# Loads, conversions and sums of logarithms moved in a fused attention and feed-forward kernel

## The chip, the cores and the metric

The kernel runs on one core of a Trainium2 chip. The core has a matrix engine (TensorE, PE in the profile, with weight loads shown as PEld), a vector engine (VectorE, DVE), a scalar engine (ScalarE, ACT), a general engine (GpSimd, POOL) and a synchronisation engine (SyncE, SP) that here issues most of the transfers. Transfers are carried by 16 DMA engines. The metric is the device time of one execution in microseconds (us).

## The reference

Two blocks run one after the other. The first is a gated linear recurrence over 768 positions, for 4 batches and 8 heads of 48 values:

```python
for t in range(S):
    state = alpha[:, :, t, :, None] * state + np.einsum('bhd,bhe->bhde', k[:, :, t], v[:, :, t])
    y[:, :, t] = np.einsum('bhd,bhde->bhe', q[:, :, t], state)
```

Its output, seen as 3072 tokens of 384 values, goes through a multiplicative feed-forward block:

```python
a = x @ w1          # 384 x 1024
b = x @ w2          # 384 x 1024
h = a * b @ w3      # 1024 x 1024
return (h @ w_out)  # 1024 x 384
```

q, k, v and alpha are float32; the four weights arrive as float64 and are read as 64-bit words.

## The kernel before, in words

**Chunks.** The positions are cut into chunks of 128: six to a batch, 24 in all (N). Within a chunk the recurrence becomes matrix products. `logs(n)` takes the logarithm of alpha on ScalarE (L233); `decays(n)` sums the logarithms along the chunk with one matmul by a triangular matrix, `utri` for odd and `after` for even chunks (L241), and ScalarE takes two exponentials of the sums (L244, L245); `decayed(n)` multiplies k and q by them on VectorE (L253); `transposed(n)` transposes both on TensorE (L272) and copies them out of PSUM on ScalarE (L273); `scores(n)` multiplies them (L311) and VectorE masks the result (L314); `outer(n)` and `advance(n)` carry the state; `attend(n)` forms the output (L330, L333), which ScalarE copies (L337) and stores to a buffer `xd` in DRAM (L343). The loop runs these functions for different chunks at once: in iteration n, `logs` works on chunk n+4, `decays` on n+3, `decayed` on n+2, `transposed` on n+1.

**Gates.** Three chunks make a group of 384 tokens. `load_x(g)` loads a group's x from `xd` into the tile xT, of which there is one (L348). `split_x(g, i)` splits it into three float32r parts: one on ScalarE (L354), two on VectorE (L355, L356), which follow each other. A gate, `gate(g, f)`, computes 128 columns of a and b for a group: twice `exact`, with six matmuls (L365), an eviction by ScalarE (L367), three more matmuls (L369) and an addition on VectorE (L370); then the product of the two (L381), stored to DRAM later (L388). `run(1)` does half a gate, one of its two `exact`s. `begin` says in which iterations a group starts: 4, 8, 12, 16 and 20, each with four gates (the last with all eight). So between two starts there are eight halves, two to an iteration.

**Conversion.** The float64 weights are turned into float32 with integer and float instructions (`to_fp32`, L184 to L194). For w1 and w2 there are twelve units (`load_gates`): each loads 2 x 256 KB (L176) and then takes four steps, the last of which write the three float32r parts (L202 to L205). `convert(steps)` advances units by so many steps. It keeps up to three units begun, that is, loaded; after a step it puts the unit back in the second place, so that two units take turns. The iterations have 3 steps up to chunk 2 and 4 after that, until the 48 steps are done. There are three buffers for the raw words.

**Order.** Loads of q, k, v, alpha, of the raw weights and of x are all issued by SP, in one queue; stores of x and of a few rows for the state (`ends`) by ScalarE. Each engine executes its instructions in a fixed order, which a scheduler sets when the program is built. The order of the text gives precedence; work that is ready is taken ahead of work that isn't. The trace shows this: the loads of w_out, which the text has after the loop, are issued from 114.76 us on.

**After the loop** the remaining gates run, mixed with the conversion of w_out and w3 and with the product w3 @ w_out (`fold`, L408 to L419), and at last `project` multiplies the stored products of a and b by that (again L365 and L369, with w3o and ab).

## Time and profile before

| | |
|---|---|
| median of 6 runs | 510.61 us (507.64 to 511.32) |
| the profiled execution, its own time | 510.45 us |
| its span, first to last instruction | 508.7 us |
| TensorE busy, matmuls and weight loads | 479.6 us (94%) and 427.5 us (84%) |
| VectorE busy | 365.6 us (72%) |
| ScalarE busy | 245.7 us (48%) |
| GpSimd busy | 12.4 us (2%) |
| DMA | 79.07 MB, 155 GB/s over the span |

The span has three stages. The loop over chunks ends at about 217 us, the remaining gates and folds at about 404 us, the projection at the end. Busy shares are averages over these stages, which have different limits. A matmul's time in the groups is longer than its share of a full pipeline: in the chain of work, six gate matmuls follow each other in 1.04 us.

### The profile page before, as it was taken

What the parts mean: (1) busy time and instruction counts of PE and PEld (TensorE: products, weight loads), DVE (VectorE), ACT (ScalarE), POOL (GpSimd) and SP (SyncE); (2) the same over time, 40 slices, a digit from 0 to 9 for tenths busy, and PEclk for the clock granted to TensorE, in tenths of its full rate; (3) what the DMA queues carried; (4) which work ended last, traced back from release to release, by engine and by line L of the source; (5) the groups of instructions that cost most, each with busy time, mean ns of one, the idle gap of its engine ahead of it and who ended that gap; (6) DMA issues with size and microseconds to landing.
All of it is one profiled execution on the core that took longest, in us unless ns stands there. A gap on an engine that the chain in (4) does not pass through costs nothing.

```text
span 508.7 us, 9463 instructions
## 1 busy us (share of the span) xinstructions
PE 479.6 (94%) x3568; PEld 427.5 (84%) x3568; DVE 365.6 (72%) x606; ACT 245.7 (48%) x465; POOL 12.4 (2%) x41
## 2 busy tenths in 40 slices
PE   3877699999899999999999999999999999999996
PEld 2655588787788888899999988898889899999996
DVE  2778799997746556499999986967434597777661
ACT  3665667666445544355555545454223433333330
POOL 1001000000000000000000000000000000000000
PEclk9989599999899999999999999999999999999999
DMA  9989999999886733165665543322100786555511
GB/s 175 181 208 204 241 214 234 236 247 231 239 147 144 156 78 98 46 185 166 198 195 162 170 158 103 125 82 69 46 32 32 197 228 193 178 175 176 172 49 46
DMA packets 168733, 79.07 MB, mean 155 GB/s; under 512 B 112856, under 2 KB 162544, under 8 KB 168688
## 3 DMA queue, kind: packets, MB, share of 16 engines
q1 hardware_dynamic: 149184, 73.68, 57.0%
q10 hardware_dynamic: 19504, 4.80, 4.8%
q8 instruction: 28, 0.46, 0.4%
q14 instruction: 17, 0.14, 0.1%
HBM read 56.40 MB, written 22.06 MB: 154 GB/s over the span
## 4 chain that ended last, share of the span: by engine, by line
PE 74%; DVE 0%; issue 0%; DVEq 0%
PE bank L365 36%; PE bank L369 18%; PE bank L414 8%; PE bank L333 2%; PE bank L272 2%; PE bank L311 2%; PE bank L408 1%; PE bank L330 1%; PE bank L283 1%; PE bank L241 1%; DVE o L370 0%; DVEq L370 0%
## 5 line engine op out<-in xcount | busy, mean ns | idle before, releaser
L365 PE MATMUL bank<-x,w 128*128 128x384 f32 x768 | 164.1, 348 | 9.6 <-ACT x L354 8.2
L365 PEld LDWEIGHTS bank<-x,w 128*128 128x128 f32 x768 | 134.5, 190 | 15.4 <-ACT x L354 8.6
L367 ACT ACTIVATE t<-bank 128x384 f32<-128x384 f32 x152 | 74.2, 491 | 129.5 <-PE bank L365 98.7
L370 DVE SCALAR_TENSOR_TENSOR r<-bank,t 128x384 f32<-128x384 f32 x128 | 69.1, 553 | 49.6 <-ACT t L367 44.4
L369 PE MATMUL bank<-x,w 128*128 128x384 f32 x384 | 88.3, 337 | 1.0 <-DVE x L356 0.9
L369 PEld LDWEIGHTS bank<-x,w 128*128 128x128 f32 x384 | 68.6, 189 | 2.3 <-DVE x L356 1.6
L365 PE MATMUL bank<-w3o,ab 128*128 128x384 f32 x384 | 70.4, 334 | 0.0
L365 PEld LDWEIGHTS bank<-w3o,ab 128*128 128x128 f32 x384 | 66.9, 188 | 0.0
L414 PE MATMUL bank<-wo,w3T 128*128 128x384 f32 x128 | 42.6, 486 | 0.0
L184 ACT ACTIVATE rest<-raw 128x512 f32<-128x512 uint32 (+1 forms) x36 | 23.5, 653 | 33.8 <-DMA raw<-in_moe_w_dram 32.2
L369 PE MATMUL bank<-w3o,ab 128*128 128x384 f32 x192 | 37.1, 334 | 0.0
L414 PEld LDWEIGHTS bank<-wo,w3T 128*128 128x128 f32 x128 | 24.2, 189 | 14.9
L381 DVE TENSOR_TENSOR ab<-r 128x384 f32<-128x384 f32 x64 | 35.5, 555 | 1.0
L314 DVE TENSOR_TENSOR ms<-bank,keep 128x512 int32<-128x512 int32 x48 | 30.9, 682 | 7.4 <-PE bank L311 7.4
L433 DVE TENSOR_TENSOR ab<-abl,ab 128x1024 fp32r<-128x1024 f32 x24 | 29.4, 1224 | 9.2 <-ACT ab L432 9.2
L432 ACT ACTIVATE ab<-abl 128x1024 fp32r<-128x1024 f32 x24 | 25.5, 1063 | 18.8 <-PE bank L369 18.8
L273 ACT COPY qkT<-bank 128x512 f32<-128x512 f32 x48 | 26.1, 588 | 16.1 <-PE bank L272 13.7
L369 PEld LDWEIGHTS bank<-w3o,ab 128*128 128x128 f32 x192 | 33.6, 188 | 0.0
L311 PE MATMUL bank<-qkT 48*128 48x128 f32 x384 | 28.9, 292 | 4.9 <-ACT qkT L273 4.9
L272 PE MATMUL bank<-ident,qk 128*128 128x128 f32 x192 | 29.3, 302 | 3.9 <-DVE qk L253 3.9
L311 PEld LDWEIGHTS bank<-qkT 48*128 48x128 f32 x384 | 24.2, 193 | 10.2 <-ACT qkT L273 6.8
L253 DVE TENSOR_TENSOR qk<-kq,e 128x768 f32<-128x768 f32 x24 | 22.9, 952 | 12.3 <-ACT e L245 7.5
(59 smaller groups left out, 499.7 us busy)
## 6 DMA issues: line engine op xcount, KB each, us to landing
abd<-ab SPq DMA_DIRECT2D x64, 192.0 KB
abl<-abd SPq DMA_DIRECT2D x24, 512.0 KB
raw<-in_moe_w_dram SPq DMA_DIRECT2D x16, 512.0 KB
xT<-xd SPq DMA_DIRECT2D x12, 576.0 KB
raw<-in_moe_w_dram SPq DMA_DIRECT2D x24, 256.0 KB
ac<-in_alpha_dram SPq DMA_DIRECT2D x24, 192.0 KB
kq<-in_k_dram SPq DMA_DIRECT2D x24, 192.0 KB
kq<-in_q_dram SPq DMA_DIRECT2D x24, 192.0 KB
```

Source lines behind the costliest of these rows:

```text
L272: nc.tensor.transpose(tp[:, ds(j * C, C)], qk[:, i, 2 * j:2 * j + 2, :], ident)
L273: nc.scalar.copy(qkT[:, i], tp.rearrange("p (j c) -> p j c", j=NP))
L311: nc.tensor.matmul(sc[i][:, j, :], qkT[r, 0, j, :], qkT[r, 1, j, :], start=True, stop=True)
L314: nc.vector.tensor_tensor(ms[:, i].bitcast(I32), sc[i].bitcast(I32), keep_bc, op=ALU.bitwise_and)
L365: nc.tensor.matmul(p1, w[part][i], x[part][i], start=(part == i == 0), stop=(part == 1 and i == n - 1))
L367: nc.scalar.activation(t, p1, AF.Copy, scale=(1.0 + 1.0 / P) * scale)
L369: nc.tensor.matmul(p2, w[2][i], x[2][i], start=(i == 0), stop=(i == n - 1))
L370: nc.vector.scalar_tensor_tensor(to, p2, -scale, t, op0=ALU.mult, op1=ALU.add)
L381: nc.vector.tensor_mul(ab, *r)
L414: nc.tensor.matmul(po, w3T[:, j, :], wo[:, j, :], start=(j == 0), stop=(j == KF - 1))
L432: nc.scalar.activation(t[:, 0], ab, AF.Copy, scale=1.0 - 2.0 ** -13)
L433: nc.vector.tensor_sub(t[:, 1], ab, t[:, 0].bitcast(FP32))
```

## The change

The diff has four parts.

- `decays(n)` for chunks from `LATE` = 10 on uses float32r. `logs` splits the logarithms into a rounded part (a copy on ScalarE) and the rest (a subtraction on VectorE), both in one tile `la2` with one buffer; `decays` makes two float32r matmuls in place of one in float32. The triangular matrices are copied once into float32r on GpSimd.
- `convert` puts a unit back in the first place, so that one unit is finished before the next is started; up to three are still loaded ahead.
- The steps of an iteration change: 3 up to chunk 2 and 4 for chunks 3 to 6, at partly other places; from chunk 7 on one, and one more in every third chunk. With the first step before the loop this makes 1 + 9 + 16 + 22 = 48 in all, the last in chunk 23.
- In the loop `load_x` is issued by ScalarE, in the iteration in which the group starts instead of at the end of the one before. The split stands in the iteration after that, behind `scores`; the first half gate of that iteration moves to its end. After the loop x is loaded by SP, as before.

```diff
+    LATE = 10
...
+    sums = p1.tile([C, 2, C], FP32R, name="sums")
...
+    nc.gpsimd.tensor_copy(out=sums[:, 0], in_=after)
+    nc.gpsimd.tensor_copy(out=sums[:, 1], in_=utri)
...
                 next(x)
-                begun.insert(min(1, len(begun)), x)
+                begun.appendleft(x)
...
-        st["la", n] = work.tile([C, DM], FP32, tag="la", name="la")
-        nc.scalar.activation(st["la", n], a, AF.Ln)
+        la = st["la", n] = work.tile([C, DM], FP32, tag="la", name="la")
+        nc.scalar.activation(la, a, AF.Ln)
+        if n >= LATE:
+
+            t = st["la", n] = work.tile([C, 2, DM], FP32R, tag="la2", name="la2", bufs=1)
+            nc.scalar.copy(t[:, 0], la)
+            nc.vector.tensor_sub(t[:, 1], la, t[:, 0].bitcast(FP32))
...
-        nc.tensor.matmul(lc, utri if n % 2 else after, st.pop(("la", n)), start=True, stop=True)
+        la = st.pop(("la", n))
+        if n < LATE:
+            nc.tensor.matmul(lc, utri if n % 2 else after, la, start=True, stop=True)
+        else:
+            for i in range(2):
+                nc.tensor.matmul(lc, sums[:, n % 2], la[:, i], start=(i == 0), stop=(i == 1))
...
-    def load_x(g):
+    def load_x(g, queue=nc.sync):
         st["xT", g] = xp.tile([C, KM, TG], FP32, tag="xT", name="xT")
-        nc.sync.dma_start(out=st["xT", g], in_=xd[g].rearrange("(k p) t -> p k t", p=C))
+        queue.dma_start(out=st["xT", g], in_=xd[g].rearrange("(k p) t -> p k t", p=C))
...
         scores(n)
+        if n - 1 in begin:
+            g, tiles = begin[n - 1]
+            split_x(g, 0)
+            fill.extend(gate(g, f) for f in tiles)
         if n == 0:
             logs(2)
             decays(2)
             logs(3)
+        early = n < 7
         convert(1, 2 if n == 0 else 3)
-        run(1)
+        run(n - 1 not in begin)
         advance(n)
         outer(n)
+        if early:
+            convert(1)
         transposed(n + 1)
         decayed(n + 2)
         logs(n + 4)
-        convert(1 if n < 3 else 2)
+        if n in begin:
+            load_x(begin[n][0], nc.scalar)
+        convert(early and n > 2)
         run(1)
         decays(n + 3)
         load_ends(n + 2)
-        convert(1)
-        if n in begin:
-            g, tiles = begin[n]
-            split_x(g, 0)
-            fill.extend(gate(g, f) for f in tiles)
+        convert(early or n % 3 == 0)
         attend(n)
-        if n + 1 in begin:
-            load_x(begin[n + 1][0])
+        run(n - 1 in begin)
     part1.close()
```

## The prediction

> **What bounds the kernel now.** I read the page's forty slices first, then the windows by stage, the waits, and the order of time around the worst gaps. The slices (12.7 us each; tenths of busy time, tenths of granted clock, busy share of the DMA engines):
>
> ```profile
> PE   3877699999899999999999999999999999999996
> PEclk9989599999899999999999999999999999999999
> DMA  9989999999886733165665543322100786555511
> ```
>
> TensorE is full from the eleventh slice to the end. The idle time lies in the first ten, where the DMA engines are full too. The windows (each engine's busy us and count, then TensorE's clock, DMA share, GB/s) show it by stage:
>
> ```profile
> 24.00:36.00 12.00, 8.03 (x118) 6.40 (x114) 7.99 (x15) 7.83 (x16) 0.91 (x3) 0.94 0.93 211
> 48.00:60.00 12.00, 4.21 (x15) 3.00 (x12) 9.20 (x14) 5.34 (x11) 0.00 (x0) 0.66 0.99 215
> 84.00:96.00 12.00, 11.42 (x123) 9.16 (x122) 11.30 (x19) 6.70 (x13) 0.77 (x2) 1.00 1.09 227
> 120.00:132.00 12.00, 9.53 (x78) 7.08 (x77) 11.41 (x22) 7.61 (x17) 0.69 (x2) 0.93 1.17 263
> 132.00:204.00 72.00, 72.00 (x771) 61.21 (x770) 41.15 (x65) 36.36 (x79) 3.80 (x10) 0.99 0.59 133
> ```
>
> From 132 us TensorE alone sets the pace (72.00 of 72); VectorE has slack there (41.15) and none at 84 to 132. The waits (engine, line, what it waited for; total, times, longest):
>
> ```profile
> PE bank L365 <- ACT x L354: 8.2, 2, 7.7
> PE bank L311 <- ACT qkT L273: 4.9, 3, 3.5
> PE bank L365 <- DVE x L355: 1.2, 1, 1.2
> ACT rest L184 <- DMA raw<-in_moe_w_dram: 32.2, 20, 3.8
> ```
>
> And the worst gaps in order of time (start, us, engine, line, [idle before, releaser]):
>
> ```profile
> 48.11 2.76 SPq L348 DMA_DIRECT2D xT<-xd  x1
> 50.76 0.53 ACT L233 ACTIVATE la<-ac 128x384 f32<-128x384 f32 x1 [2.66 <-DMA ac<-in_alpha_dram]
> 54.60 1.17 ACT L354 ACTIVATE x<-xT 128x1152 fp32r<-128x1152 f32 x1 [1.27 <-DMA xT<-xd]
> 55.82 2.72 PE L365 MATMUL bank<-x,w 128*128 128x384 f32 x6 [7.69 <-ACT x L354]
> ...
> 121.16 0.49 ACT L367 ACTIVATE t<-bank 128x384 f32<-128x384 f32 x1 [4.79 <-DVE power L188]
> ```
>
> The first gate stands in TensorE's order right behind chunk 5's scores and waits 7.69 us: x came to SP's turn only at 48.11, behind the inputs, and landed at 54.6. At 121 ScalarE stood 4.79 us still: its next conversion (L184, of w_out) had no data, and evictions stood behind it.
>
> To price each place I take the starts of the attention's output matmuls (L333). Undisturbed chunks with two gate halves are 8.36 us apart (144.34, 152.70, 161.06), and 7.6 to 7.8 where a batch begins or ends. Chunk 12 to 13 took 13.19 (122.79 to 135.98), a loss of 4.8; chunk 8 to 9 took 9.82, a loss of 1.5; chunk 2 to 6 took 42.8 (29.54 to 72.34), where two gateless chunks at 5.55 (23.99 to 29.54), one of 7.6 and one of 7.76 make 26.5, a loss of 16.3.
>
> **What the Trainium skill says.** "TensorE: Matmul & The Clock Gate", The HAM clock gate: an idle window of about 3.4 us halves the clock until about 3.4 us of work have passed. The trace agrees: after the 7.69 us gap the clock reads 0.50 from 52 to 62 us, so that gap costs some 3 us more. "FP8 and Floating Point Precision", TensorE Precision Notes: true fp32 takes four passes. The trace agrees in time: 0.64 us for 384 columns (below) against 0.173 for one fp32r matmul. "DMA: Bandwidth & Descriptors", Queues, rings and completion order: SP and ACT each own a row of rings, and a DMA engine goes round the rows; its section Issuing engines are not separate DMA queues adds that this gives no bandwidth. So x on ScalarE's row need not stand behind SP's backlog but shares its rate; no x load on that row is in this trace.
>
> **Sums of logarithms, chunks 10 to 23.** The price stands in TensorE's order with and without them:
>
> ```profile
> 159.21 0.68 PE L369 MATMUL bank<-x,w 128*128 128x384 f32 x3
> 159.73 0.81 PE L241 MATMUL bank<-la,utri 128*128 128x384 f32 x2
> 160.46 0.67 PE L330 MATMUL bank<-qkT,T 48*64 48x128 f32 x16
> ...
> 199.62 0.69 PE L369 MATMUL bank<-x,w 128*128 128x384 f32 x3
> 200.23 0.67 PE L330 MATMUL bank<-qkT,T 48*64 48x128 f32 x16
> ```
>
> L369 to L330 takes 1.25 us with the sum and 0.61 without: 0.64 for the fp32 pair. Two fp32r matmuls of the same 128x384 at the gates' pace (six in 1.04 us on the chain: 0.173 each) take 0.35. Gain 0.29; fourteen sums, issued in chunks 7 to 20, where TensorE is the bound: 4.1 us. Added: a ScalarE copy of 128x384 (0.49 to 0.53 by L417 and L233) and a VectorE subtraction (0.555, L381), 7 us and 7.8 us in all, hidden: each has a chunk between logs(m) and decays(m), and both engines idle over 40% after 132 us. At chunks 7 to 12 VectorE has no slack now (11.30 of 12); there the slower conversion must pay for it. If that cover were gone, 6 x 0.555 = 3.3 us. The two GpSimd copies at the start (128x128, 0.2 to 0.3 us each by its memsets; at most 1) are needed at chunk 7: nothing.
>
> The new tile la2 has one buffer: the copy for chunk n+4 waits for the matmuls of decays(n+3), which stand behind the middle gate half. Behind it on ScalarE stand the exponentials and evictions. The exponentials are wanted a chunk later, so I take nothing; the ends are nothing and, at worst, the slower rival below.
>
> **Conversion.** Work is unchanged: twelve units of four steps, 48 in all. VectorE's share of a unit is 0.41+0.41+0.68+0.68+0.68+0.70+0.68 = 4.2 us, so four steps a chunk make 4.2, beside 5.0 for attention, gates and split: 9.2 against TensorE's 8.36. From chunk 7 the text gives 1.3 steps (1.4 us): 6.4, with the new subtraction 7.0, under 8.06. Raw traffic falls from 512 KB a chunk to about 170. The text sets only precedence: w_out's loads, written after the loop, were issued at 114.76, so idle slots will take conversions early; half the relief may go that way.
>
> One unit at a time changes the lead. Alternating, units finish in pairs and the sixth is loaded at step 16 and used at step 18; in sequence every later load has eight steps. That is the 32.2 us of ScalarE's waiting, one case of which stopped TensorE for 3.5 us at 34 us. Steps until chunk 6 are the same, 26.
>
> **x and its split.** Five loads leave SP's queue (0.4 to 2.8 us each there) for ScalarE's: five issues there of about 0.4 us, up to 1 [...] (its own stores take 0.4 to 1). They wait for x's stores, with evictions queued behind. The split now stands behind scores of the next chunk, and the gate half that needs it behind the outer product (0.6) and transposes (0.83); the half left out follows the attention. The gates' count in the loop stays 38 halves. The split's chain is 1.17 + 1.27 + 1.27; later splits were already taken as soon as the old x3 was free (159.92) and hidden, and stay so. Both ends for all five together: 3 us lost, 8 gained, the latter counted in the places below.
>
> **The sum.** Sums 4.1. Chunk 13: 4.0 of 4.8 (no w_out blockage in that stage, VectorE freer). Chunk 9: 1.0 of 1.5. Chunks 3 to 6: the stall goes, but transfers limit. To reach chunk 10's alpha, which ScalarE reads in chunk 6, 38 input tiles of 192 KB, 7 raw units of 512, six stored x, one loaded x and one ab make 13.1 MB; at the 193 GB/s of 0 to 48 us and 229 of 48 to 64, that is 65 us. Chunk 6's attention at some 66.3 instead of 72.34 is a gain of 6 of 16.3; ends 0 and 12. New issues and waits on ScalarE: minus 0.6. Total 14.5. The later stages (512 KB weights, projection) are TensorE-bound with the same work: nothing; about 7 us of w_out conversion now done early may come later, into a stage where VectorE is busy 12 of 12 (216 to 228) but later idles 40%. Span 508.7 - 14.5 = 494.2; with the 1.75 around it (510.45) 495.95, and 0.16 more for the median (510.61): 496 us.
>
> **Rivals.** (1) The early stage stays transfer-bound: the DMA share at 0.99 speaks for it, the dips to 62 GB/s at 50 to 52 against. Without the 6: 502. (2) The waits merely move; conversions fill in as before and stall behind raw data: only sums less issues, 3.5: 507. (3) All gaps go, 4.1+16.3+1.5+4.8 = 26.7: 484; the 65 us above speak against. (4) Slower: la2's single buffer. ScalarE stops in each of fourteen chunks until decays(n+3) is through, and the transposes' copies behind it stop TensorE. It decides from 14.5/14 = 1.04 us a chunk; at 1.5 us the loss is 21, net 517. For it: ScalarE already waits 98.7 us for gate matmuls. Against: its order shows work moved around such waits.
>
> **Numbers.** Forecast 0.50 (own range 491 to 500), rivals 0.20, 0.12, 0.08, 0.10. Range 487 to 507.5: it leaves out (3)'s far end, (4), and the tails. No change means within 0.3%, 509.1 to 512.1, about what a measurement of this kernel can tell. Faster 0.87, same 0.04, slower 0.09.
>
> **What would show it.** Right: L241 in fp32r at 0.35 a pair and full periods near 8.06; x on ACTq before 50 us and no 7 us gap before the first gate; 12 to 13 under 9.5; raw waits on L184 well under 32. Wrong: TensorE waiting on the transposes' copies in every chunk from 7 on, ScalarE standing on x's stores, or logs in chunks 4 to 6 waiting for alpha longer than now.

## The result and the profile after

The changed kernel takes 508.68 us (median of 35 runs, 506.05 to 510.85) beside 509.93 us for the kernel before (72 runs, 506.51 to 514.17). The ratio is 0.998, with a 95% interval of 0.9967 to 0.9993. The forecast of 496 us is missed, and the time lies outside the range too. The profiled execution took 509.62 us and its span is 507.7 us; before, it was 510.45 and 508.7. Of all the runs below, one, of the sums with small transfers on GpSimd (509.09 us), was in a slower state of the chip and is left out of its ratio. Lines of the changed kernel stand 5 to 15 further down: the gate matmuls are L380 and L384 (before L365 and L369), the split of x L369 to L371 (before L354 to L356), the conversion's first operation L189 (before L184).

The forty slices of the page after, as before (TensorE, its granted clock, the DMA engines):

```profile
PE   3987599999799999999999999999999999999997
PEclk9989599999799999999999999999999999999999
DMA  9989999999977833155664543321100776555511
```

The dip around 50 us (fifth slice) is still there, and the one in the eleventh slice, 127 to 140 us, is deeper, in TensorE and in its clock (7 tenths each, 8 before). The windows by stage (busy us and count of TensorE, its weight loads, VectorE, ScalarE, GpSimd; clock; DMA share; GB/s):

```profile
24.00:36.00 12.00, 10.41 (x152) 8.22 (x148) 8.43 (x17) 7.92 (x17) 0.91 (x3) 0.96 0.94 204
48.00:60.00 12.00, 5.52 (x33) 4.18 (x34) 9.39 (x14) 7.23 (x14) 0.00 (x0) 0.67 1.02 219
84.00:96.00 12.00, 11.03 (x125) 9.15 (x128) 8.63 (x15) 7.77 (x16) 0.80 (x2) 1.00 1.08 217
120.00:132.00 12.00, 7.88 (x72) 5.61 (x71) 12.00 (x21) 8.48 (x17) 2.12 (x3) 0.94 1.17 259
132.00:204.00 72.00, 72.00 (x773) 62.62 (x771) 48.26 (x82) 40.57 (x90) 3.76 (x10) 0.96 0.61 138
```

In 120 to 132 us TensorE fell from 9.53 to 7.88, and VectorE, which was to be freed there, is busy for the whole 12.00. After 132 us TensorE is full, but its clock is 0.96 where it was 0.99. The waits:

```profile
ACT rest L189 <- DMA raw<-in_moe_w_dram: 24.2, 15, 3.5
ACT la L238 <- DMA ac<-in_alpha_dram: 14.9, 6, 3.6
PE bank L380 <- ACT x L369: 7.3, 2, 5.6
```

The wait for raw weights fell from 32.2 to 24.2 us. TensorE's wait for the split fell from 8.2 to 7.3 only.

The starts of attention's output matmuls show where the time went. A full chunk takes 8.05 us in the changed kernel (153.65 to 161.70) and 8.36 before.

| from chunk to chunk | before, us | after, us | difference |
|---|---|---|---|
| start of the span to 4 | 45.58 | 46.23 | +0.65 |
| 4 to 8 | 43.46 | 42.70 | -0.76 |
| 8 to 12 | 33.75 | 32.69 | -1.06 |
| 12 to 14 | 21.55 | 23.97 | +2.42 |
| 14 to 23 | 70.22 | 68.48 | -1.74 |
| 23 to the end of the span | 294.14 | 293.63 | -0.51 |
| span | 508.7 | 507.7 | -1.0 |

The cheaper sums gain where TensorE is full (8 to 12 and 14 to 23). The stall of chunks 3 to 6 hardly shrank, and that of chunk 13 grew.

**Chunk 5.** ScalarE, its queue (ACTq) and TensorE in order of time (start, us, engine, line, [idle before, releaser]):

```profile
42.69 0.39 ACTq L363 DMA_DIRECT2D xT<-xd  x1
...
51.47 0.52 ACT L238 ACTIVATE la<-ac 128x384 f32<-128x384 f32 x1 [3.63 <-DMA ac<-in_alpha_dram]
...
54.48 1.17 ACT L369 ACTIVATE x<-xT 128x1152 fp32r<-128x1152 f32 x1
...
55.70 1.33 PE L380 MATMUL bank<-x,w 128*128 128x384 f32 x3 [5.62 <-ACT x L369]
```

x was asked for at 42.69, where SP's turn came only at 48.11 before. Yet the split starts at 54.48, as it did before (54.60): ScalarE stood 3.63 us for alpha of chunk 8, and then did the logarithm, two operations of a conversion step, two exponentials and two copies of the output, which stand ahead of the split in its order.

**Chunk 13.** The same engines, 120 to 132 us:

```profile
121.65 0.63 ACT L207 ACTIVATE w<-mant 128x512 fp32r<-128x512 f32 x1 [0.57 <-DVE mant L199]
...
123.13 0.69 ACT L189 ACTIVATE rest<-raw 128x512 f32<-128x512 uint32 x1
...
124.08 0.73 ACT L194 ACTIVATE power<-power,rebias 128x512 uint32<-128x512 uint32 x1
...
126.56 1.17 ACT L369 ACTIVATE x<-xT 128x1152 fp32r<-128x1152 f32 x1
...
127.78 0.79 PE L380 MATMUL bank<-x,w 128*128 128x384 f32 x3 [1.70 <-ACT x L369]
130.08 0.87 PE L380 MATMUL bank<-x,w 128*128 128x384 f32 x3 [1.51 <-DVE x L370]
131.44 1.30 PE L384 MATMUL bank<-x,w 128*128 128x384 f32 x3 [0.49 <-DVE x L371]
```

ScalarE works without a pause from 121.65 to the split, and three of those operations (2.05 us) are steps of conversion units that the text places many chunks later. VectorE has the same units before L370, with no gap from 114.98 to 132.2 us. By 123.8 us eleven of the twelve units of w1 and w2 were done, and SP had issued the first load of w_out at 116.77; the text places the twelfth unit's end in chunk 23. So the order that was built took the conversions earlier than the text has them. In the kernel before, though, all twelve had ended at 115.9 us, ahead of chunk 13: beside it the change moved the last two units back, and in front of this split.

**The sums.** TensorE in a full chunk, the place shown before:

```profile
144.04 0.68 PE L384 MATMUL bank<-x,w 128*128 128x384 f32 x3
144.56 0.50 PE L256 MATMUL bank<-la,sums 128*128 128x384 f32 x2
145.00 0.67 PE L345 MATMUL bank<-qkT,T 48*64 48x128 f32 x16
```

L384 to L345 takes 0.96 us instead of 1.25: the 0.29 of the forecast.

### The profile page after: what moved, and what is told of

Same layout as the page of the kernel before. It is cut to its first block, busy times and chain, and to the rows that moved or that the text cites. A ratio compares the mean times of both kernels' runs of the same rounds, so it can differ in the third digit from the quotient of the medians.

```text
span 507.7 us, 9496 instructions
## 1 busy us (share of the span) xinstructions
PE 480.7 (95%) x3568; PEld 429.3 (85%) x3568; DVE 371.6 (73%) x620; ACT 250.7 (49%) x479; POOL 16.7 (3%) x43
## 4 chain that ended last, share of the span: by engine, by line
PE 73%; DVE 1%; issue 0%; DVEq 0%
PE bank L380 37%; PE bank L384 18%; PE bank L429 8%; PE bank L348 2%; PE bank L326 2%; PE bank L287 2%; PE bank L423 1%; PE bank L345 1%; PE bank L298 1%; PE bank L256 1%; DVE x L371 0%; DVE x L370 0%; DVE o L385 0%; DVEq L385 0%
## 5 line engine op out<-in xcount | busy, mean ns | idle before, releaser
L380 PE MATMUL bank<-x,w 128*128 128x384 f32 x768 | 163.4, 347 | 9.7 <-ACT x L369 7.3
L380 PEld LDWEIGHTS bank<-x,w 128*128 128x128 f32 x768 | 133.9, 190 | 16.2 <-ACT x L369 7.8
L384 PE MATMUL bank<-x,w 128*128 128x384 f32 x384 | 88.7, 339 | 1.3 <-ACT la L238 0.7
L384 PEld LDWEIGHTS bank<-x,w 128*128 128x128 f32 x384 | 68.9, 190 | 2.8 <-PE bank L380 1.4
L380 PE MATMUL bank<-w3o,ab 128*128 128x384 f32 x384 | 70.4, 334 | 0.0
L380 PEld LDWEIGHTS bank<-w3o,ab 128*128 128x128 f32 x384 | 66.9, 188 | 0.0
L384 PE MATMUL bank<-w3o,ab 128*128 128x384 f32 x192 | 37.1, 334 | 0.0
L429 PEld LDWEIGHTS bank<-wo,w3T 128*128 128x128 f32 x128 | 24.2, 189 | 14.9
L189 ACT ACTIVATE rest<-raw 128x512 f32<-128x512 uint32 (+1 forms) x36 | 23.4, 651 | 26.1 <-DMA raw<-in_moe_w_dram 24.2
L384 PEld LDWEIGHTS bank<-w3o,ab 128*128 128x128 f32 x192 | 33.6, 188 | 0.0
L385 DVE SCALAR_TENSOR_TENSOR o<-bank,t 128x384 f32<-128x384 f32 x24 | 13.4, 557 | 22.4 <-issue 14.4
```

Source lines behind the costliest of these rows:

```text
L380: nc.tensor.matmul(p1, w[part][i], x[part][i], start=(part == i == 0), stop=(part == 1 and i == n - 1))
L384: nc.tensor.matmul(p2, w[2][i], x[2][i], start=(i == 0), stop=(i == n - 1))
L385: nc.vector.scalar_tensor_tensor(to, p2, -scale, t, op0=ALU.mult, op1=ALU.add)
L429: nc.tensor.matmul(po, w3T[:, j, :], wo[:, j, :], start=(j == 0), stop=(j == KF - 1))
```

## The experiments

Each ratio is to executions of the kernel before that ran beside the kernel in question. Their median went from 509.46 to 510.60 us from one group of experiments to the next, so a difference of medians between two groups is uncertain by about 1 us, and the ratios are the safer measure. Single executions of one kernel lie 2 to 4 us to either side of its median, so medians and ratios decide on time, and the chunk intervals of the one profiled execution say where. That execution is not always a typical one: it is the slowest of its kernel for "sums" (504.77 us), for "six units not loaded" (507.98) and for "sums, steps, small transfers on GpSimd" (508.29), and the fastest for "sums, split, steps" (506.02). The three intervals shown hold most of what differs; where the start or the chunks after 14 count, the text says so. At 8.05 us a chunk they would be 32.2, 32.2 and 16.1 us. Chunks 5, 9 and 13 are the split chunks: in each the first half gate of a new group needs x's split.

| kernel | median, us | ratio, 95% | 4 to 8 | 8 to 12 | 12 to 14 |
|---|---|---|---|---|---|
| before | 509.93 | 1 | 43.46 | 33.75 | 21.55 |
| after (sums, turns, split, steps) | 508.68 | 0.998 [0.9967, 0.9993] | 42.70 | 32.69 | 23.97 |
| sums | 503.40 | 0.9867 [0.9839, 0.9896] | 40.88 | 32.31 | 19.91 |
| sums, steps | 503.79 | 0.9871 [0.9837, 0.9905] | 40.06 | 32.62 | 17.94 |
| sums, turns | 509.35 | 0.9985 [0.9972, 0.9998] | 43.75 | 38.17 | 17.51 |
| sums, split | 508.23 | 0.9960 [0.9940, 0.9979] | 40.61 | 40.75 | 16.85 |
| sums, turns, steps | 510.28 | 1.0011 [0.9992, 1.0030] | 41.89 | 35.96 | 21.92 |
| sums, split, steps | 509.04 | 0.9985 [0.9967, 1.0002] | 39.48 | 36.45 | 20.09 |
| sums, turns, split | 510.39 | 1.0002 [0.9982, 1.0022] | 43.91 | 36.33 | 17.50 |
| after, logarithms one chunk later | 513.01 | 1.0066 [1.0041, 1.0090] | 36.29 | 37.34 | 21.89 |
| after, fewer loads of v | 504.34 | 0.9889 [0.9846, 0.9931] | 43.16 | 30.82 | 20.41 |
| after, x split once | 507.86 | 0.9957 [0.9938, 0.9977] | 42.92 | 37.39 | 17.04 |
| after, six units not converted | 505.98 | 0.9905 [0.9867, 0.9943] | 43.20 | 39.20 | 16.08 |
| after, six units not loaded | 505.91 | 0.9918 [0.9889, 0.9947] | 43.03 | 31.53 | 23.07 |
| after, six units held back | 510.15 | 0.9991 [0.9971, 1.0010] | 43.11 | 30.83 | 22.46 |
| sums, steps, six units held back | 509.63 | 0.9973 [0.9955, 0.9991] | 39.62 | 31.23 | 24.29 |
| after, small transfers on GpSimd | 511.24 | 1.0026 [1.0005, 1.0047] | 40.71 | 34.62 | 21.52 |
| sums, small transfers on GpSimd | 502.07 | 0.9840 [0.9797, 0.9884] | 39.85 | 32.08 | 19.19 |
| sums, steps, small transfers on GpSimd | 505.29 | 0.9923 [0.9903, 0.9944] | 41.85 | 34.51 | 22.62 |
| after, six filling matmuls | 505.83 | 0.9939 [0.9920, 0.9958] | 41.98 | 32.47 | 20.12 |

The parts are named so: *sums* is the float32r sums, *turns* one conversion unit at a time, *split* x's load, split and half gate in their new places, *steps* the new step counts.

### Which part of the change does what

The sums alone, on the kernel before:

```diff
+    LATE = 10
...
+            for i in range(2):
+                nc.tensor.matmul(lc, sums[:, n % 2], la[:, i], start=(i == 0), stop=(i == 1))
```

> The kernel before with the float32r sums of logarithms alone. Theory A (the sums are worth their TensorE time, 14 x 0.29 = 4.1 us, wherever TensorE sets the pace): 505.5 to 507 where the kernel before has 510. Theory B (the copy and the subtraction that they add at chunks 7 to 12, where VectorE has no idle time, take the gain back): 508.5 or more, with a longer gap between chunks 12 and 13 than the 13.2 us of the kernel before.

503.40 us, 6.5 us less than the kernel before. The sums were worth more than their 4.1: the profiled execution is also 2.6 us shorter from chunk 4 to 8 and 1.6 from 12 to 14, which the price of the matmuls does not explain; that the built order came out better is likely and was not tested by itself. The other three parts together therefore cost 5.3 us. First each was taken out of the changed kernel. The split:

```diff
         scores(n)
-        if n - 1 in begin:
-            g, tiles = begin[n - 1]
-            split_x(g, 0)
...
-            load_x(begin[n][0], nc.scalar)
...
+        if n in begin:
+            g, tiles = begin[n]
+            split_x(g, 0)
...
         attend(n)
-        run(n - 1 in begin)
+        if n + 1 in begin:
+            load_x(begin[n + 1][0])
```

> The changed kernel with the load of x, the split and the half gate where the kernel before has them, and x loaded by SP. Theory C (the moved split is what takes the gain back: it stands later in the orders of ScalarE and VectorE): 1.5 to 4 us faster than the changed kernel, chunk 12 to 14 at 21 to 22 us instead of 24.0. Theory D (VectorE's backlog is what stops chunk 13, wherever the split stands): within 1 us of the changed kernel. For the first gate both expect no gain: about 5 to 8 us of idle TensorE before it, since ScalarE waits for the alpha of chunk 8 in either.

510.28 us. The turns:

```diff
-                begun.appendleft(x)
+                begun.insert(min(1, len(begun)), x)
```

> The changed kernel with two conversion units taking turns again. As the prediction had it (the eight steps' lead removes stalls): 1 to 3 us slower than the changed kernel. If inputs, not conversions, set the early stage: within 1 us of it, and the attention of chunk 6 at 71 to 73 us in both.

509.04 us (the profiled execution, 506.02, is at the fast end of its runs, so its early chunks count for little). The steps:

```diff
-        convert(early and n > 2)
+        convert(1 if n < 3 else 2)
...
-        convert(early or n % 3 == 0)
+        convert(1)
```

> The changed kernel with the steps of conversion of the kernel before (3 up to chunk 2, then 4, to chunk 12). Theory D (VectorE is full until chunk 13 because the scheduler takes conversions early whatever the text says): within 1 us of the changed kernel, and the last conversions of w1 and w2 no more than 20 us earlier than in it. The prediction (fewer steps free VectorE): 2 us or more slower.

510.39 us. Taking one out gives nothing back, so no single part owns the loss. Then each was added to the sums alone:

```diff
-                begun.insert(min(1, len(begun)), x)
+                begun.appendleft(x)
```

> The float32r sums and one conversion unit at a time; x's load, split and half gate stand where the kernel before had them, and the step counts are the old ones. Theory P (the order of the units is what eats the gain of the sums, since a unit that is taken up is run to its end on a full VectorE): about 509, 5 to 6 us over the 503.4 of the sums alone, with the extra time between the attend steps of chunks 8 and 14 (near 57 us where the sums alone have 52.2). Theory Q (any change of the order in which ScalarE and VectorE meet their work brings the stall back; no part owns it): 507 to 511 here and in both of the other single parts. Theory R (the moved split owns it): no more than 504.5 here.

509.35 us. The split:

```diff
         scores(n)
+        if n - 1 in begin:
+            g, tiles = begin[n - 1]
+            split_x(g, 0)
...
+            load_x(begin[n][0], nc.scalar)
...
         attend(n)
+        run(n - 1 in begin)
```

> The float32r sums and the moved load, split and half gate of x (load on ScalarE's queue in the chunk of the split's group, split and half a gate one chunk later); the old alternation of units and the old step counts. Theory P (order of units): no more than 504.5. Theory Q (any change of order): 507 to 511. Theory R (the moved split owns the loss: ScalarE issues one more transfer behind its x stores, and half a gate is late in its chunk): about 509, and the attend step of chunk 14 at 144 us or later, where the sums alone have 140.2.

508.23 us. The steps:

```diff
-        convert(1 if n < 3 else 2)
+        convert(early and n > 2)
...
-        convert(1)
+        convert(early or n % 3 == 0)
```

> The float32r sums and the new step counts (fewer from chunk 7 on), old alternation, x's load and split as before. With three units begun in turn and fewer steps from chunk 7, less VectorE work is put into chunks 8 to 14. Theory P: no more than 504.5, perhaps a little under 503.4. Theory Q: 507 to 511. Theory R: no more than 504.5. That two of the three single parts each come out at 507 or more would say that the loss is one stall that several edits bring on, since taking out any one of the three left 509 to 510.

503.79 us. The turns alone cost 5.9 us and the split alone 4.8; the steps cost nothing (503.79 beside 503.40). Theory P has the turns right and the split wrong, theory R the split right and the turns wrong. What neither has is that most of the loss comes with either part alone, and that the two don't add up: together, without the steps, they cost 7.0 us. Theory Q went too far, since the steps are free.

Both stall in chunk 9, at the split, for different reasons. With the turns (ScalarE and TensorE in order of time):

```profile
89.02 0.52 ACT L237 ACTIVATE la<-ac 128x384 f32<-128x384 f32 x1 [2.76 <-DMA ac<-in_alpha_dram]
...
93.00 1.18 ACT L367 ACTIVATE x<-xT 128x1152 fp32r<-128x1152 f32 x1
...
94.24 0.79 PE L378 MATMUL bank<-x,w 128*128 128x384 f32 x3 [2.52 <-ACT x L367]
```

ScalarE stood for alpha ahead of the split. With the split moved (ScalarE, its queue, VectorE, TensorE):

```profile
90.71 1.18 ACT L369 ACTIVATE x<-xT 128x1152 fp32r<-128x1152 f32 x1
...
91.76 2.84 ACTq L358 DMA_DIRECT2D xd<-x  x2
94.65 0.67 ACT L189 ACTIVATE rest<-raw 128x512 f32<-128x512 uint32 x1 [2.76 <-DMA xd<-x]
...
95.61 1.34 DVE L370 TENSOR_TENSOR x<-xT,x 128x1152 fp32r<-128x1152 f32 x1
...
97.01 0.80 PE L380 MATMUL bank<-x,w 128*128 128x384 f32 x3 [2.69 <-DVE x L370]
```

Here ScalarE was held by two of its own stores, which took 2.84 us to issue, but its part of the split had run before them, at 90.71. What the half gate waited for was VectorE's part, at 95.61. VectorE had stood 2.29 us for raw weights at 88.42, and from 90.59 it worked without a pause on conversion steps, the rest of a logarithm, a gate, the decayed k and q and the masks, all ahead of the split in its order.

### Chunk 5: what was late

```diff
             decays(2)
-            logs(3)
...
-        logs(n + 4)
+        logs(n + 3)
```

> The changed kernel with the logarithms of chunk n + 3 instead of n + 4 in chunk n, so that ScalarE asks for alpha one chunk later and no longer stands 3.6 us for alpha of chunk 8 ahead of the first split of x. Theory: alpha's arrival and not x's load held the first split in chunk 5; then the split (at 54.5 us in the changed kernel) starts by 51.5, the attend step of chunk 6 (72.1 us) comes 2 to 5 us earlier, and if nothing later takes it back the time is 504 to 507. Rival: the early stage is bound by what the input transfers bring as a whole, so the wait only moves to another tile of the same chunk (k and q for the exponentials' product): attend of chunk 6 within 1 us of 72.1, time within 1 us of 508.7.

The split of the first group as ScalarE ran it:

```profile
50.01 1.16 ACT L369 ACTIVATE x<-xT 128x1152 fp32r<-128x1152 f32 x1 [0.92 <-DMA xT<-xd]
```

It starts 4.5 us earlier, and what it now waits for is x, 0.92 us. The attend step of chunk 6 comes at 69.65 instead of 72.12, and chunks 4 to 8 take 36.29 instead of 42.70. So in the changed kernel alpha, not x, held the split. But chunk 4 itself came 4.3 us later (50.51), and chunks 8 to 14 gave back 2.5: 59.2 us instead of 56.7. The median is 4.3 us above the changed kernel's, against the expectation. The profiled execution (510.84 us) is a fast one of its kernel. The gain ahead of chunk 8 was lost again here.

### Chunks 8 to 14: transfers, engines or the split

```diff
-            nc.sync.dma_start(out=st["v", n][:, :, 0:D], in_=rows(v, n))
+            if n < len(vs):
+                nc.sync.dma_start(out=st["v", n][:, :, 0:D], in_=rows(v, n))
```

> The changed kernel with v loaded for the first five chunks only (later chunks read these again; the result is then not the reference's): 3.7 MB less of the some 31 MB that move before 144 us, everything else in its order. Theory T (up to chunk 14 the transfers as a whole set the pace, and the stalls only say where the deficit shows): at some 225 GB/s 3.7 MB are 16 us of transfers, so the attend step of chunk 14 comes at 139.5 us or earlier instead of 145.6, and the time is 502 or less. Theory W (the stall of chunk 13 is the chain of the split, ScalarE to VectorE to TensorE, behind engines that are full or stand in their own queue): attend of chunk 14 between 143.5 and 147.5, time 506.5 to 510.

The attend step of chunk 14 came 5.4 us earlier (140.22), the time is 504.34. That is a third of the 16 us of transfers taken away: between the two theories, so transfers are a part of the cause and not the pace.

```diff
-            split_x(g, 0)
+            if g == 0:
+                split_x(g, 0)
+            st["x3", g] = st["x3", 0]
```

> The changed kernel with x split once in the first part, for group 0; the gates of groups 1 to 4 read that split again (the result is then not the reference's). The loads of x stay, so the transfers are the same; 1.17 us of ScalarE and 2.7 us of VectorE are gone in each of chunks 9, 13, 17 and 21, and with them TensorE's wait for the split. Theory W: the stall of chunk 13 (1.70 + 1.51 + 0.49 us of waits and the half clock behind them) goes, attend of chunk 14 at 141 us or earlier, time 504 or less. Theory T: the stall moves to another tile; attend of chunk 14 within 1.5 us of 145.6, time 507 to 510.

507.86 us, and chunk 14 at 143.58. Chunk 13's stall is gone (12 to 14 in 17.04), but chunk 9 has one, which no split can make. VectorE and TensorE there:

```profile
96.98 0.43 DVE L190 TENSOR_SCALAR mant<-raw 128x512 uint32<-128x512 uint32 x1 [2.87 <-DMA raw<-in_moe_w_dram]
97.32 1.28 DVE L329 TENSOR_TENSOR ms<-bank,keep 128x512 int32<-128x512 int32 x2
...
98.06 1.71 PE L345 MATMUL bank<-qkT,T 48*64 48x128 f32 x16 [3.17 <-DVE ms L329]
```

VectorE stood 2.87 us at a conversion (L190) whose raw weights had not landed, and the masks behind it held TensorE. Theory T, under which the stall moves to another tile, has this run's time (507 to 510) and nearly its place. Of theory W the stall of chunk 13 goes, but neither chunk 14 nor the time follows.

The two halves of a conversion unit were then taken apart, for the six units that the first gates don't need. Loaded, not converted:

```diff
+        if c0 >= CW:
+            raw = rawp.tile([C, 2 * n], I64, tag="raw", name="raw")
+            for i, src in enumerate((moe_w1, moe_w2)):
+                nc.sync.dma_start(out=raw[:, ds(i * n, n)], in_=src[ds(kk * C, C), ds(c0, n)])
...
+            return
```

> The changed kernel with the last six units loaded but not converted (their part of the weights is zero, so the result is not the reference's): some 4 us of VectorE and 2 us of ScalarE fewer for each, the transfers as before. If VectorE's and ScalarE's time is the share of theory D that counts: attend of chunk 14 at 141 us or earlier, time 503.5 or less. If the transfers are: within 2 us of 145.6. Theory E: within 1.5 us of 145.6.

Converted from a constant tile, not loaded:

```diff
-        raw = rawp.tile([C, n], I64, tag="raw", name="raw")
-        for i, src in enumerate(srcs):
+        raw = raw0 if late else rawp.tile([C, n], I64, tag="raw", name="raw")
+        for i, src in enumerate(srcs if not late else ()):
```

> The changed kernel with the last six units converted from a constant tile, without their loads (3.1 MB less; the result is not the reference's): the work of VectorE and ScalarE stays, 3.1 MB of transfers go. The 3.7 MB of v taken away before brought the attend step of chunk 14 forward by 5.4 us. If transfers are the share that counts: 4 to 6 us earlier again (139.5 to 141.5), time 502.5 to 505. If the engines' time is: within 2 us of 145.6, or later, since units without a load to wait for are ready sooner and pressed in earlier.

Without the conversions' work chunks 12 to 14 take 16.08 us, with no loss at all; without their loads 23.07, nearly the changed kernel's 23.97. That fits the trace of chunk 13 above, where the time of these units on ScalarE and VectorE stands in front of the split. So do the sums with the turns, with the split, and with both: the twelfth unit ended at 122.8, 125.9 and 127.2 us there, ahead of chunk 13's split, and chunks 12 to 14 took 16.9 to 17.5. With the steps, where most of the last two units' work came behind that split, they took 17.94. One rival is left: all three, and the run without the work, had a long stretch from 8 to 12 (36.3 to 40.8 us), and a stall there may leave less to lose in chunk 13. Nor is it what the kernel gains as a whole: from chunk 8 to 14 the two take 55.3 and 54.6 us, and both run in some 506 us, about 3 less than the change. Without the work another stall came, in chunk 10, ScalarE and TensorE:

```profile
114.29 0.55 ACT L191 ACTIVATE rest<-raw 128x384 f32<-128x384 uint32 x1 [7.50 <-DMA raw<-in_moe_w_out_dram]
...
115.57 1.01 PE L268 MATMUL bank<-la,sums 128*128 128x384 f32 x2 [4.53 <-DVE ms L341]
```

With six units out of the way the built order took conversions of w_out early instead. ScalarE, held for 1.88 us by its own stores at 110.26, stood 7.50 us in all before such a conversion, evictions and copies waited behind it, and TensorE stood 4.53 us.

So the six units were held back by a true dependence, an output of chunk 11, in the changed kernel and in the sums with the steps:

```diff
+        if "gate" in st:
+            nc.gpsimd.tensor_copy(out=raw.bitcast(FP32)[:, 0:1], in_=st["gate"])
...
-        early = n < 7
+        early = n < 7 or n > 11
```

> The changed kernel with the last six of the twelve conversion units of w1 and w2 really held back: their loads and work hang on an output of chunk 11, and the steps go up again from chunk 12. The first gates use only the first six. Theory D (what makes the deficit between chunks 8 and 14 is that these six units, 3.1 MB of loads and some 4 us of VectorE and 2 us of ScalarE each, are still done there although the text spreads them to chunk 23): attend of chunk 14 at 141 us or earlier instead of 145.6, chunk 12 to 14 in less than 20 us; the time 504 or less, unless the units are then late for the gates of chunk 17 on, which would show as TensorE waiting there. Theory E (the deficit is no matter of these units): attend of chunk 14 within 1.5 us of 145.6, time 507 to 511.

> The float32r sums and the new step counts, with the last six units held back until chunk 11 as above and the steps up again from chunk 12; old alternation, x as before. The sums with the steps alone lost 2.3 us against full chunks between 8 and 14. Theory D: attend of chunk 14 at 134.5 to 137 us instead of 136.8, time 499 to 503.8, with little left to gain. Theory E: within 1.5 us of 503.8.

In the changed kernel chunk 14 came at 140.45, 5.1 us earlier, as theory D has it, and the time is still 510.15. Chunks 8 to 12 lose nothing (30.83), but the units then crowd into chunk 13 (22.46 for 12 to 14) and into chunk 17, where chunks 16 to 18 take 19.8 us instead of 14.9, again with TensorE standing at the split (1.14 and 1.77 us for VectorE's parts), not for late weights. In the sums with the steps, which lost 1.8 us in chunks 12 to 14 before, 12 to 14 takes 24.29 us and the median is 5.8 us higher. Holding the units back moved their work into a split chunk in both.

### ScalarE's own transfers

```diff
-            nc.scalar.dma_start(out=to[half, :, :, ds(c * C, C)], in_=x[ds(DP * half, D)])
+            nc.gpsimd.dma_start(out=to[half, :, :, ds(c * C, C)], in_=x[ds(DP * half, D)])
```

The three stores of ends' rows and the load of the decays move in the same way.

> The changed kernel with the small transfers of the first part (stores of x, rows of ends, loads of the decays) issued by GpSimd instead of ScalarE; only the loads of x stay on ScalarE. Theory I (ScalarE stands in its own transfer issues, 4 to 5 us of them between 50 and 100 us and as many up to 145, and the evictions and the split wait behind them): attend of chunk 14 at 141.5 us or earlier, time 504.5 or less. Theories T and W: the issues move, the deficit stays; attend of chunk 14 within 1.5 us of 145.6, time 507 to 510. If GpSimd is slow to issue, the products on it that make the decayed state come late: then over 510, with TensorE waiting for T.

> The kernel before with the float32r sums alone, and the small transfers (stores of x, rows of ends, loads of the decays) on GpSimd's queue. Theory I: the stall of chunk 12, where ScalarE issued for 2.09 us and then stood 3.21 us, goes: attend of chunk 14 at 137.5 us or earlier instead of 140.2, time 501 or less. Theories T and W: within 1.5 us of 503.4. A slow issue on GpSimd: over 505.

> A version made of what cost nothing alone: the float32r sums, the new step counts, and the small transfers of the first part on GpSimd; alternation and x's load and split as before. If the gains stand beside each other: 499 to 503, loss against full chunks between 8 and 14 no more than 2.5 us. If the order is as sensitive as with the other pairs of edits, one of the stalls of chunk 9 or 13 comes back at 3 us or more, and the time is 504 to 509.

In the changed kernel this is 2.6 us slower than the change itself, and chunk 14 comes at 148.28: what theory I forecast there did not come. But the edit brought a stall of its own, and chunk 4 came 5.2 us later (51.43). GpSimd, ScalarE's queue and TensorE:

```profile
40.39 1.24 POOL L315 TENSOR_TENSOR dec<-dec 128x4 f32<-128x4 f32 x1 [5.23 <-DMA dec<-ends]
...
47.78 0.38 ACTq L363 DMA_DIRECT2D xT<-xd  x1
...
48.79 1.65 PE L253 MATMUL bank<-la,utri 128*128 128x384 f32 x2 [7.18 <-ACT la L238]
```

GpSimd stood 5.23 us for the decays and issued the stores of x behind that, at 42.20 and 43.82. ScalarE's load of x, which reads what these stores write, was issued only at 47.78, the next logarithm stood behind it, and TensorE waited 7.18 us for that (for T only 0.5 us in all). So this run doesn't say what ScalarE's own issues cost in the changed kernel. Beside the sums alone, where SP loads x, it is the fastest median of all, 502.07, but 1.3 us is less than the two intervals can tell apart. With the steps as well the time is 505.29, and in the profiled execution the stall of chunk 13 is back (22.62): two edits that cost nothing alone cost 1.5 us together, though the two intervals just touch. The version to keep is the sums alone, 1.3% faster than the kernel before and 1.0% faster than the changed one.

### The clock behind a stall

```diff
+            for _ in range(warm if part == 0 else 0):
+                nc.tensor.matmul(p2, w[0][0], x[0][0], start=True, stop=True)
...
+                  6 if i == f == 0 and g < 4 else 0)
```

> The changed kernel with six more matmuls of 0.17 us (1.04 us) on the first part of the split in the first half gate of groups 0 to 3, whose result is overwritten: TensorE has work while VectorE still makes the second part. The lost time of chunks 12 to 14 in the changed kernel is 7.9 us: 4.0 of idle time and 3.4 of a clock of 0.86 over 24 us; in other kernels the clock's share was 1.7, 3.4 or 5.3, as if lost in portions of 1.7 us. Theory K (a portion of the clock is lost for a stretch of idle time, and is as large as the idle time itself): the idle time behind VectorE's second part falls by about 1 us and one portion goes, so chunk 12 to 14 takes 21.3 to 22.5 us instead of 24.0, the time 505.5 to 508. Rival: the clock follows the long wait alone, or nothing in the idle time: the six matmuls only take up idle time, chunk 12 to 14 stays within 0.7 us of 24.0, time 508 to 510.

The windows between the attend steps of chunks 12 and 14, first the changed kernel:

```profile
121.62:145.59 23.97, 19.91 (x185) 16.14 (x184) 19.20 (x35) 14.79 (x32) 3.39 (x5) 0.86 0.93 194
```

and with the six filling matmuls, whose result is overwritten:

```profile
119.05:139.17 20.12, 17.91 (x191) 15.02 (x191) 15.69 (x29) 12.27 (x26) 2.62 (x5) 1.00 0.94 195
```

The clock of 0.86 over 23.97 us is 3.4 us of TensorE's time, and all of it came back: 1.00. That is no accident of one execution: over the whole span the clock was 0.983 to 0.990 in the 21 executions with the filling and 0.972 to 0.983 in the 35 of the changed kernel. TensorE with the filling:

```profile
124.35 0.79 PE L380 MATMUL bank<-x,w 128*128 128x384 f32 x3 [0.85 <-ACT e L260]
124.98 1.20 PE L382 MATMUL bank<-x,w 128*128 128x384 f32 x6
126.03 0.68 PE L380 MATMUL bank<-x,w 128*128 128x384 f32 x3
127.71 0.78 PE L386 MATMUL bank<-x,w 128*128 128x384 f32 x3 [1.00 <-DVE x L371]
```

The six run where TensorE stood 1.51 us for L370. The time is 505.83 us, 2.9 less than the change (2.1 by the ratios), though 4.2 us of extra matmuls are issued in four chunks. Theory K holds, with two portions saved instead of one; part of the 3.85 us may be that the wait for ScalarE was shorter in this execution (0.85 beside 1.70). The edit also builds a new order: chunk 4, ahead of all filling, came 1.6 us earlier, and chunks 14 to 23 took 2.0 us more, of which the filling is 1.04. How much of the 2.9 us is the clock's was not tested apart from that.

## Why the prediction was wrong

**Sums, 4.1 us: right.** A pair takes 0.29 us less, as forecast; where TensorE is full, from chunk 14 to 23, the span shrank by 1.74 (the seven sums there should give 2.0). The new operations on ScalarE and VectorE and the single buffer of la2 cost nothing that shows: alone, the part gave 6.5 us. Rival 4 is out.

**Chunks 3 to 6, 6 us of 16.3: wrong.** The failing step is "x came to SP's turn only at 48.11, behind the inputs, and landed at 54.6" taken as the thing to mend, and the estimate from 13.1 MB of transfers as the next limit. The load did move ahead, to 42.69, and the split did not (54.48). The lines that I showed say why: ScalarE stood only 1.27 us for x ahead of the split, and the wait for alpha, 2.66 us at 50.76, stood in front of the split in the same queue; it grew to 3.63 us and became the limit. The run with the logarithms one chunk later shows it: the split at 50.01.

**Chunk 13, 4.0 us of 4.8: wrong in sign.** Chunks 12 to 14 became 2.4 us longer: 12 to 13 took 12.75 instead of 13.19, 13 to 14 took 11.22 instead of 8.36. Two steps failed. First, the 4.79 us at 121 were read as "its next conversion (L184, of w_out) had no data", and as what chunk 13 lost. The orders of ScalarE, VectorE and TensorE in the kernel before say otherwise:

```profile
115.18 0.68 DVE L205 SCALAR_TENSOR_TENSOR w<-w,mant 128x512 fp32r<-128x512 f32 x1
...
116.41 2.14 ACTq L343 DMA_DIRECT2D xd<-x  x2
120.07 0.36 DVE L185 TENSOR_SCALAR mant<-raw 128x384 uint32<-128x384 uint32 x1 [2.28 <-DMA raw<-in_moe_w_out_dram]
...
120.20 0.86 ACTq L261 DMA_DIRECT2D dec<-ends  x2
...
121.55 0.54 ACT L184 ACTIVATE rest<-raw 128x384 f32<-128x384 uint32 x1
...
126.02 0.79 PE L365 MATMUL bank<-x,w 128*128 128x384 f32 x3 [0.53 <-ACT x L354]
127.98 0.80 PE L365 MATMUL bank<-x,w 128*128 128x384 f32 x3 [1.18 <-DVE x L355]
129.25 0.79 PE L369 MATMUL bank<-x,w 128*128 128x384 f32 x3 [0.47 <-DVE x L356]
```

L184 comes after ScalarE's wait, not in it. In the gap ScalarE issued two stores of x for 2.14 us and came to the loads of the decays only at 120.20. This profile doesn't count an issuing engine as busy, and puts its idle time down to the last event. A conversion of w_out did wait for its data, but on VectorE (L185, 2.28 us), and TensorE had work meanwhile. What TensorE stood for in chunk 13 was the three parts of x's split, 0.53, 1.18 and 0.47 us, and the lower clock behind them took 1.7 us more; in the changed kernel it stood for the same three, longer (1.70, 1.51 and 0.49). (That an early conversion of w_out can hold ScalarE is true in kind: it did so for 7.50 us in an experiment.) Second, "VectorE freer": the forecast warned that half the relief might go to conversions taken early, and then counted on the relief. All of it went: VectorE was busy 12.00 of 12. The twelfth unit of w1 and w2 had ended at 115.9 us before (L205); now the last two ended at 123.8 and 143.8, so the slower conversion put their steps into chunk 13, ahead of the split on both engines. The experiments on the six units fit that, with the one rival named there.

**Chunk 9, 1.0 us: not there.** Chunks 8 to 12 are 1.06 us shorter in the profiled execution, but four sums of 0.29 are 1.16, and the forecast counted these apart; chunk 8 to 9 fell from 9.82 to 7.52 and chunk 9 to 10 rose from 8.35 to 9.95. "Minus 0.6" for x's load on ScalarE was far too little: the split's move alone costs 4.8 us beside the sums, and in its trace VectorE's part of the split is late for the half gate. The forecast's lower end for that part, a loss of 3 us, was not carried to the sum.

**The conversion's lead** was misread in size. By the text of `convert` the sixth unit is loaded ahead of step 15 and first used at step 19 when units take turns, a lead of four steps and not two; one unit at a time does give eight. The waits for raw weights fell by 8 of 32.2 us, but beside the sums alone the turns cost 5.9 us.

**The rival that came nearest** is the second, that the waits merely move, at 507 us. What it lacked was that a stall can grow where it lands, and that the clock nearly doubles it. The first rival, an early stage bound by transfers, has the missing 6 us right but not for its reason: with fewer loads of v chunks 4 to 8 took 43.16 us, no less than 42.70.

**The method.** The sum priced each place from the trace of before and let the edits act on it. But all engines' orders are built anew from the whole text, and an edit moves waits in chunks that it does not touch: beside the sums alone the turns put 5.9 us into chunks 8 to 12, and the steps took 2.0 from 12 to 14. What stays open is why these edits give just these orders. The experiments show what each order stalls on, not how it was chosen.

## What to carry to other kernels

In this kernel's first part several engines and the transfers are all near full, and there a stall was not owned by the instruction that TensorE waited for: where it was taken away, the next late transfer or crowded engine made another. In such a place, take the edit that shortens the bound engine's own work first and alone, and test every reordering beside it separately, since here two of three cost what the sums had gained. Before a wait is put down to data that are late, read everything that stands ahead of it in that engine's queue, its own transfer issues included.

## What the runs showed that was not expected

- The clock's price comes in portions. Between 70 and 500 us the low stretches of the clock, at 0.50, are 3.41 us or whole multiples of that in these traces, so that a portion is 1.7 us of TensorE's time: one before and with the sums alone (12 to 14), two in the changed kernel (12 to 14) and with the turns (8 to 12), three with the split (8 to 12; three are 5.1 us, and the 5.3 of the last experiment's expectation is a clock rounded to 0.87). The Trainium skill ("TensorE: Matmul & The Clock Gate", The HAM clock gate) has the clock halved in windows of about 3.4 us, and the traces agree. The page has it halved after an idle window; here TensorE was idle for no longer than 1.70 us at a time in chunk 13, and a partly idle window was enough. In the changed kernel, the window ahead of the low stretch and the stretch's first window (TensorE busy 1.35 and 2.92 us, clock 1.00 and 0.50):

```profile
127.23:130.64 3.41, 1.35 (x6) 0.94 (x6) 3.41 (x5) 1.96 (x4) 0.59 (x2) 1.00 1.10 296
130.64:134.05 3.41, 2.92 (x23) 2.19 (x21) 2.70 (x7) 1.13 (x3) 0.82 (x1) 0.50 1.22 233
```

- In the same place TensorE was busy for 1.80 us of the window before and 2.04 with the sums alone, and a low stretch followed; with the sums and steps the emptiest window had 2.22 and with the filling 2.41, and none did. That fits six matmuls buying back 3.4 us. It is not a fixed limit: a window with 1.95 us busy at 41.9 in the changed kernel was followed by none. The page also says that the windows run free, which would let the same idle time fall into one window or be shared by two; no run here tests that.
- Issuing a transfer can take long. The skill ("DMA: Bandwidth & Descriptors", Issuing engines are not separate DMA queues) calls the time that a sequencer takes to initiate a transfer usually small beside the transfer. Here two stores of x took 2.84 us to issue on ScalarE (sums and split, at 91.76) and one of k's loads 4.34 us on SP (at 44.32 in the changed kernel), where landing takes 5.4 in the median; no eviction ran on ScalarE in those 2.84 us.
- A filling matmul can pay: with 1.04 us of useless work in each of four chunks the kernel was 2.9 us faster (2.1 by the ratios).
